# One pair of batch 1's queries and keys from TensorE transposes to DMA transposes, in a kernel of local attention and SwiGLU on one Trainium2 core

## The chip, the cores and the metric

The kernel runs on one core of one Trainium2 chip. The metric is device time in microseconds (us), taken over whole executions of the program; a second execution is recorded by the hardware profiler, and from it come the profile page and the trace. Lower is better. The engines of the core go by the profile's names: PE is TensorE (matrix products), PEld its weight loads, DVE is VectorE, ACT is ScalarE, POOL is GpSimd, SP is SyncE. POOL issues the loads that convert float32 to float16 on the way (software DMA); SP, and ACT for a few, issue the others.

## What is computed

An attention over 4 batches of 8 heads, 768 positions, 64 values per head, and a feed-forward block on its result. Each position sees the first 8 positions (the global keys) and the 96 positions up to itself:

```python
is_global = pos[None, :] < 8
is_local = (rel >= 0) & (rel < 96)          # rel = query position - key position
dist = np.where(is_global & ~is_local, 96.0, np.abs(rel))
scores = q @ k.T / 8 - slope[head] * dist    # slope = 2 ** -(head + 1)
scores = np.where(is_global | is_local, scores, -1e9)
a = softmax(scores)                          # over the keys, 1e-9 added to the sum
x = (a @ v) as (4 * 768, 8 * 64) = (3072, 512)
g = x @ w_gate                               # (512, 1536)
out = (g * sigmoid(g) * (x @ w_val)) @ w_out # (1536, 512), out (3072, 512) float32
```

Inputs and output are float32 in the chip's memory.

## The kernel before

**Staging.** Everything that TensorE multiplies is float16. Keys and queries must lie with the 64 values of a head across the partitions; two heads (a pair, `hp` 0 to 3) fill the 128 partitions. kT[hp] holds a pair's keys in 7 chunks of 120 with the 8 global keys ahead of each, qT holds its 768 queries. There are three ways to fill them:
- Batch 0 is loaded in halves of 384 positions and transposed on TensorE (`T`, tr_half, L360; products L364), then copied out of PSUM with a change of order (`k`, keys_half; `q`, queries_half, copy at L393). Its first pairs come as float32 through the queues of ACT and SP (`Lf`) and are cast (`cast`, L347).
- Pairs 0 and 1 of batch 1 come as two loads of four heads (`L4`, ld_four, L293) and are transposed on TensorE, 12 transposes for each call (`U`, tr_whole, L398; products L402), then copied out by `kw` (keys_whole, L406) and `qw` (queries_whole, L417).
- Pairs 2 and 3 of batch 1, and all of batches 2 and 3, come one head at a time by rows (`Lr.b.i.h`, ld_rows, L304, issued at L305; i is 0 for keys, 1 for queries). A DMA transpose on SP's queue (`D.b.hp.i`, tr_dma, L423, issued at L430) writes queries straight to qT and keys to kN, from which DVE spreads them into kT (`K`, spread_keys, L434).

The staging tiles, kst for keys and qst for queries, have two buffers each and are taken in turn by batch 0's float32, batch 0's float16, and batches 1, 2 and 3 (L290). Batch 3's first load of keys therefore goes into the buffer that batch 1's keys lie in, and waits for its last reader. kN and qT have four buffers each.

V comes in seven chunks per batch (`Lv.b.c`, ld_v, L264, issued at L267), with the V rows of the global keys copied into each chunk afterwards (`G`, put_globals; `G.1.1.7.S` is a DMA on SP that does chunks 1 to 6 of batch 1). The three vS tiles are cleared where no rows come (`Z`). The weights come in 256 KB pieces (`Lw.which.n.g`, ld_w, L312; which is 0 for w_gate, 1 for w_val) and w_out in three of 512 KB (`Lo`). `Lw.1.0.1` is the second half of the first 512 columns of w_val.

**Attention.** `c.b.hp.u` (scores, L481) multiplies keys by queries into two PSUM banks, `x` (exps, L526) takes the exponent on ACT into one of the at-buffers, `m` (mask, L553) multiplies by the mask on DVE. The masks hold exp(-slope * distance), made by ACT (`M.head.part`, L335); some units of batch 0 get the distance added by TensorE instead (`B`, L461, from `sl`). `w.b.g.half.what` (weigh, L571, products L585) sums over keys for four heads (g) and 384 queries (half): what 0 gives the sums of the weights, with `ones` (made by `pre`, L323) as left operand, 1 and 2 give even and odd columns of the weighted V. `i` (invert, transpose L604) and `r` (spread, L608) turn the sums into reciprocals in the right places, `n` (take_num, L597) copies weighted sums out of PSUM on ACT where the banks are wanted, and `p` (scaled, L621) writes the product, a quarter of a tile of x, transposed as xT.

**Feed-forward.** x is done in 8 tiles t of 384 positions, two per batch. For each of 12 blocks f of 128 columns there are four products with w_gate (`g.t.f`; `ga` and `gb` are its first and second half) and four with w_val (`v.t.f`), all at L638; ACT takes a tanh (`t`), DVE makes the rest of the gate (`s`) and the product with the value (`h`). `o.t.i.part` (L679, for the last rows L668) multiplies 128 rows by w_out, `e.t.i` (put_out) scales and stores them: on ACT and SP (L697), and for the last 128 rows e.7.2 on ACT's own queue and e.7.3 by DVE (L692) with the store on SP (L693).

**What sets the order.** Nothing is scheduled by the compiler. The string ORDER (L39 to L123) lists every step as name and arguments, the table WORK (L702) gives the function of each name, and the steps are issued in that order; each engine and each queue runs its own in order, waiting only for data and for buffers. The letter at the end of some steps is the engine: V is DVE, A is ACT, P is POOL, S is SP. The 8 PSUM banks are dealt by `single` and `double` in the order of the steps, so a moved step can also get another bank. `fill` (L343) runs products on a bank of no use, 14 and later 2, ahead of the first transposes.

```python
    for step in ORDER.split():
        name, *args = step.split(".")
        WORK[name](*(int(a) if a.isdigit() else a for a in args))
```

Batch 0's attention comes first, its second half among the first feed-forward tile; batch 1's loads are issued during tiles 0 and 1, its transposes, scores and sums stand in tile 1 and between tiles 1 and 2; batches 2 and 3 follow in the same way.

## Time and profile before

| | before |
|---|---|
| median of 3 runs | 238.46 us (238.38 to 238.53) |
| the profiled execution | 238.79 us, of it 237.0 from the first to the last instruction (the span) |
| granted TensorE clock | 1.0 |
| ACT: tanh (L644) | 96 instructions, 491 ns each, 44.1 us |
| DVE: gate (L648) and product (L654) | 96 each, 547 and 551 ns, 50.8 and 51.3 us |
| PE: products with w_gate and w_val (L638) | 384 each, 72.1 and 73.3 us |
| PE: products with w_out (L679) | 276, 68.5 us |
| DMA | 25.54 MB, 108 GB/s on the mean, 162 to 207 GB/s in the slices of the first quarter |
| V loads (Lv) | 24 of 120 KB, 8.0 us from issue to landing (median) |
| key and query rows (Lr) | 20 each, of 96 KB, 7.9 and 8.5 us |

In a row of the trace the first numbers are the start and the length in us, then come the engine, the line, the operation, the tile written and the tile read; "x4" is a group of four. What stands in square brackets is idle time of the engine ahead of the instruction and what ended it. In the chain of waits each row is a start, a length and a piece of work that the end of the span depended on. In a row by stretches of time the first column is the stretch and its length, followed by the busy times of PE, PEld, DVE, ACT, POOL and SP, the granted clock, and the DMA engines' load (the last number is GB/s). A queue's row ("SPq") is the issuing of a transfer; the transfer lands later, and a row of DMA issues gives the KB of each and the time from issue to landing. Times on POOL are rough.

### The profile page before, as it was taken

How to read it: one execution, taken by the hardware profiler on the slowest of the kernel's cores; microseconds unless marked ns; L12 is line 12 of the kernel's file. 1: busy time of each engine (PE TensorE's matmuls, PEld its weight loads, DVE VectorE, ACT ScalarE, POOL GpSimd, SP SyncE). 2: the span in 40 equal slices, each digit the busy share in tenths (PEclk: the TensorE clock that was granted, in tenths of full speed). 3: DMA queues.
4: the chain of work that ended last, by engine and by line, in shares of the span. 5: the costliest groups of instructions: out<-in, count | busy, mean ns of one | idle time of the engine just before them, and what ended most of it. 6: DMA issues, size and time to landing. Idle time of an engine off the chain costs nothing.

```text
span 237.0 us, 6183 instructions
## 1 busy us (share of the span) xinstructions
PE 229.5 (97%) x2520; PEld 132.3 (56%) x2520; DVE 173.8 (73%) x428; ACT 138.0 (58%) x251; POOL 77.6 (33%) x102
## 2 busy tenths in 40 slices
...
GB/s 177 181 182 207 193 198 186 176 176 162 139 130 153 178 165 139 141 167 112 139 192 55 44 80 27 20 47 47 0 44 48 3 1 0 44 47 0 8 125 177
DMA packets 88196, 25.54 MB, mean 108 GB/s; under 512 B 78016, under 2 KB 85224, under 8 KB 88168
## 3 DMA queue, kind: packets, MB, share of 16 engines
...
q8 instruction: 19, 0.31, 0.5%
...
## 4 chain that ended last, share of the span: by engine, by line
PE 94%; DVE 3%; ACT 1%; issue 1%; DVEq 0%
PE banks L638 53%; PE banks L679 26%; PE banks L585 6%; PE banks L481 4%; PE banks L343 2%; PE banks L668 1%; PE banks L364 1%; ACT at L526 1%; PE banks L461 1%; PE banks L402 1%; DVE at L518 0%; DVE rb L611 0%; DVE at L517 0%; DVE dT L604 0%; DVE xT L621 0%
## 5 line engine op out<-in xcount | busy, mean ns | idle before, releaser
L644 ACT ACTIVATE th<-banks 128x384 f32<-128x384 f32 x96 | 44.1, 491 | 60.1 <-PE banks L638 54.6
L638 PE MATMUL banks<-xT,wv 128*128 128x384 f16 x384 | 73.3, 326 | 0.0
L638 PE MATMUL banks<-xT,wg 128*128 128x384 f16 x384 | 72.1, 326 | 0.0
L654 DVE TENSOR_TENSOR hT<-banks,sl 128x384 f16<-128x384 f32 x96 | 51.3, 551 | 24.0 <-PE banks L638 22.2
L679 PE MATMUL banks<-wo,hT 128*128 128x512 f16 x276 | 68.5, 379 | 0.0
L526 ACT ACTIVATE at<-banks 64x640 f16<-64x640 f32 (+4 forms) x88 | 62.3, 714 | 5.3 <-PE banks L481 4.3
L648 DVE SCALAR_TENSOR_TENSOR sl<-th,banks 128x384 f32<-128x384 f32 x96 | 50.8, 547 | 12.6 <-ACT th L644 11.6
L638 PEld LDWEIGHTS <-wg 128*128 128x128 f16 x384 | 37.3, 98 | 27.0
L638 PEld LDWEIGHTS <-wv 128*128 128x128 f16 x384 | 36.4, 98 | 26.6
L679 PEld LDWEIGHTS <-hT 128*128 128x128 f16 x276 | 26.1, 98 | 26.5
L553 DVE TENSOR_TENSOR at<-at,masks 128x864 f16<-128x864 f16 (+5 forms) x62 | 26.1, 459 | 4.5 <-ACT at L526 4.4
L267 POOL DMA_DIRECT2D vS<-in_v_dram x28 | 25.0, 899 | 10.3 <-DMA vS<-in_v_dram 3.0
L697 ACT ACTIVATE osb<-banks 128x512 f32<-128x512 f32 x23 | 13.6, 597 | 22.1 <-PE banks L679 18.4
L305 POOL DMA_DIRECT2D kst<-in_k_dram x20 | 16.7, 841 | 14.1 <-DMA kN<-kst 8.8
L305 POOL DMA_DIRECT2D qst<-in_q_dram x20 | 16.8, 846 | 7.5 <-DMA qst<-in_q_dram 2.6
L481 PE MATMUL banks<-qT,kT 64*64 64x160 f16 (+9 forms) x408 | 13.3, 227 | 0.2 <-DVE xT L621 0.2
L481 PEld LDWEIGHTS <-kT 64*64 64x64 f16 (+1 forms) x408 | 7.9, 104 | 8.9 <-issue 7.6
L621 DVE TENSOR_TENSOR xT<-ns,rb 128x384 f16<-128x384 f32 x24 | 12.5, 550 | 0.3
L585 PE MATMUL banks<-at,vS 128*32 128x216 f16 (+6 forms) x576 | 12.0, 225 | 0.1
L597 ACT COPY ns<-banks 128x768 f32<-128x768 f32 x12 | 9.4, 801 | 4.5 <-PE banks L585 4.2
L604 DVE STREAM_TRANSPOSE dT<-banks 128x384 f32<-128x384 f32 x16 | 9.2, 574 | 3.1 <-PE banks L585 2.8
L585 PEld LDWEIGHTS <-vS 128*32 128x32 f16 x576 | 10.0, 95 | 2.3 <-issue 1.5
...
## 6 DMA issues: line engine op xcount, KB each, us to landing
out_dram<-osb SPq DMA_DIRECT2D x23, 256.0 KB, 2.1
...
qst<-in_q_dram POOLq DMA_DIRECT2D x20, 96.0 KB, 8.5
kst<-in_k_dram POOLq DMA_DIRECT2D x20, 96.0 KB, 7.9
wg<-in_moe_w_gate_dram POOLq DMA_DIRECT2D x6, 256.0 KB, 9.3
wv<-in_moe_w_val_dram POOLq DMA_DIRECT2D x6, 256.0 KB, 8.3
...
```

The source lines that it names most:

```text
L267: nc.gpsimd.dma_start(out=v_of(b)[r0:r0 + n, c, :, :], in_=v[b, :, KC * c:KC * c + n, :].rearrange("h p d -> p h d"))
L305: nc.gpsimd.dma_start(out=rows_of(i, b, h // 2)[:, :, h % 2, :], in_=KQ[i][b, h].rearrange("(t p) d -> p t d", p=128))
L481: nc.tensor.matmul(sc[k0:k1, hi, col + a:col + z], lhsT=keys[r, k0:k1], rhs=qTs[b, hp][r, q0 + a:q0 + z], start=fresh, stop=True, skip_gro ...
L526: nc.scalar.activation(out=of(at), in_=of(sc), func=AF.Exp, scale=scale)
L553: ENG[e].tensor_mul(a2, a2, m[:, :, m0:m0 + n])
L585: nc.tensor.matmul(dst[r, o:o + n], lhsT=vSs[b][:, c, 4 * g + j, what - 1::2] if what else ones[:, 0:32], rhs=ats[b, hp, u][:, j % 2, col: ...
L638: nc.tensor.matmul(gv[t, f, which][:, 0:TB], lhsT=w[:, c, 128 * f:128 * f + 128], rhs=xTs[t][:, c, :], start=(c == 0), stop=(c == NC - 1))
L644: nc.scalar.activation(out=th, in_=gv[t, f, 0][:, 0:TB], func=AF.Tanh, scale=0.5)
L648: nc.vector.scalar_tensor_tensor(out=sl, in0=gv[t, f, "t"], scalar=1.0, in1=gv[t, f, 0][:, 0:TB], op0=AluOp.add, op1=AluOp.mult)
L654: nc.vector.tensor_mul(hTs[t][:, f, :], gv[t, f, 1][:, 0:TB], gv[t, f, "s"])
L679: nc.tensor.matmul(ops_t[t, i], lhsT=hTs[t][:, f, 128 * i:128 * i + 128], rhs=wo[:, f, :], start=(f == 0), stop=(f == NFF - 1))
L697: nc.scalar.mul(out=osb, in_=ops, mul=0.5)
```

## The change

Pair 1 of batch 1 now takes the third way: its heads 2 and 3 come by rows (Lr.1.0.2, Lr.1.0.3, Lr.1.1.2, Lr.1.1.3), D.1.1.0 and D.1.1.1 transpose them by DMA, and K.1.1 spreads the keys. The steps U.1.0, U.1.1, kw.1 and qw.1 are gone, and so is n.1.1.0. Pair 0 alone stays on TensorE; its load takes two heads, not four.

```diff
-    def ld_four(i, h0):
+    def ld_pair(i, hp):
         nc.gpsimd.dma_start(
-            out=stage(1, i)[:, h0:h0 + 4, :],
-            in_=KQ[i][1, h0:h0 + 4].rearrange("h (p j) d -> p h (j d)", p=128))
+            out=stage(1, i)[:, 2 * hp:2 * hp + 2, :],
+            in_=KQ[i][1, 2 * hp:2 * hp + 2].rearrange("h (p j) d -> p h (j d)", p=128))
...
-        "G": put_globals, "Z": clear_rest, "L4": ld_four, "Lr": ld_rows,
+        "G": put_globals, "Z": clear_rest, "L2": ld_pair, "Lr": ld_rows,
```

The whole of ORDER is new. ORDER takes one line more, so the functions behind it stand one line lower than before (L638 is L639). Beside the steps above, these are the same steps at other places, but for the engine of five: cast.1.0 and k.3.1 go to DVE, q.1.0, q.0.0 and q.1.1 to ACT. What changes most:
- In the opening `pre` comes first. Seven of the sixteen masks (M.0.0, M.1.0, M.2.0, M.3.0, M.4.0, M.6.0, M.7.0), the clearing of the at-buffers' corners (zc.1, zc.2) and of two V tiles (Z.1, Z.2) go behind the first feed-forward products.
- On POOL's queue, Lr.3.0.1 stands ahead of Lv.1.1 to Lv.1.6; before, Lv.1.0, Lv.1.1, Lv.1.3 and Lv.1.2 stood ahead of it.
- On SP's queue, G.1.1.7.S stands behind D.2.0.0 and the stores e.0.0 and e.0.1.
- At the end e.7.2 stands ahead of e.7.1.

Of ORDER, the opening, the stretch in which batch 1 begins, and the end (some lines are left out at "..."):

```diff
-Ld.S Z.0.P Z.3.P Lf.A.1.1 Li zc.0.V Lh.0.0.4.8 zc.1.V Lf.A.1.0 Lh.1.0.4.8 pre cast.1.1.V Lf.S.0.1
-M.5.1 M.0.0 sl.3 Lf.S.0.0 M.2.1 Lh.1.1.0.4 fill.14 sl.7 M.1.0 sl.6 Lh.0.1.0.4 Z.1.V sl.2 cast.0.1.V
-M.7.0 T.1.0.1 B.1.1 q.1.0.V M.3.1 cast.1.0.P T.1.0.0 Lh.1.1.4.8 cast.0.0.A M.2.0 fill.2 Lv.0.1
-k.1.0.V sl.1 M.7.1 T.0.0.0 T.2.0.0 k.0.0.V Lv.0.0 T.3.0.0 sl.0 k.3.0.V M.4.1 M.5.0 B.1.0 M.0.1
-T.0.0.1 c.0.1.1 Lh.0.1.4.8 sl.4 T.2.0.1 M.3.0 c.0.1.0 q.0.0.V x.0.1.1 Lv.0.2 q.2.0.V T.1.1.1 T.3.0.1
-M.6.0 B.0.0 k.2.0.V x.0.1.0 Lv.0.3 c.0.0.0 sl.5 M.1.1 Lw.0.0.1 c.0.0.1 T.1.1.0 x.0.0.1 q.3.0.V M.4.0
-T.0.1.1 B.2.0 k.1.1.V c.0.2.0 Lw.0.0.0 B.3.1 x.0.0.0 Lw.1.0.0 x.0.2.0 Lw.1.0.1 M.6.1 T.0.1.0 q.1.1.V
-m.0.0.1.V w.0.0.0.0 Lw.0.1.0 B.3.0 k.0.1.V q.0.1.A c.0.3.1 x.0.3.1 c.0.2.1 c.0.3.0 i.0.0.0 Lw.0.1.1
-zc.2.V r.0.0.0 B.0.2 c.0.0.2 x.0.2.1 T.3.1.0 T.3.1.1 m.0.2.1.V T.2.1.1 x.0.3.0 Lw.1.1.1 w.0.1.0.0
-x.0.0.2 G.0.1.4.V k.3.1.A c.0.1.3 w.0.0.0.1 i.0.1.0 Lw.1.1.0 q.2.1.A w.0.0.0.2 T.2.1.0 w.0.1.0.1
-p.0.0.0.0.V x.0.1.3 w.0.1.0.2 r.0.1.0 k.2.1.A p.0.0.0.1.V c.0.2.2 Lw.0.2.0 c.0.0.3 q.3.1.A ga.0.0
-x.0.2.2 p.0.1.0.0.V ga.0.2 p.0.1.0.1.V G.0.4.7.S m.0.1.3.V c.0.1.2 x.0.0.3 c.0.2.3 Lw.0.2.1 Lv.0.6
-Lv.0.5 Lv.0.4 gb.0.2 x.0.1.2 gb.0.0 t.0.2 ga.0.1 m.0.2.2.V Lw.1.2.1 m.0.0.3.V gb.0.1 v.0.1 m.0.1.2.V
-w.0.0.1.0 s.0.2 t.0.0 s.0.0 c.0.3.3 Lw.1.2.0 x.0.2.3 i.0.0.1 c.0.3.2 v.0.0 g.0.3 t.0.1 x.0.3.3
...
-g.0.6 Lr.1.1.6 Lo.0 Lv.1.0 v.0.6 G.1.1.7.S Lv.1.1 m.0.2.3.V m.0.3.3.V Lo.1 h.0.1 v.0.5 s.0.7 t.0.6
-s.0.5 Lr.1.0.6 v.0.7 Lv.1.3 g.0.11 s.0.6 h.0.3 Lr.1.1.4 h.0.5 t.0.4 s.0.4 h.0.7 Lr.1.0.5 m.0.3.2.V
...
-v.0.9 p.0.1.1.1.V Lr.2.0.0 v.0.10 g.0.8 v.0.11 g.1.4 g.1.6 t.0.8 D.1.2.0 s.0.8 h.0.9 Lr.2.0.1 g.1.1
-h.0.10 t.1.4 t.1.1 h.0.2 g.1.8 s.1.4 g.1.5 s.0.11 U.0.0 U.0.1 D.1.2.1 s.1.1 U.1.1 t.1.8 U.1.0
-Lr.1.0.7 h.0.11 v.1.4 s.1.8 t.1.6 kw.0.A v.1.6 qw.1.A kw.1.V g.1.0 s.1.6 v.1.8 h.1.4 qw.0.A h.1.6
-t.1.0 Lv.1.2 s.1.0 c.1.0.1 c.1.1.0 v.0.8 g.1.9 t.1.5 h.1.8 x.1.1.0 s.1.5 t.1.9 x.1.0.1 v.1.1 g.1.2
-h.0.8 o.0.1.0 D.1.3.0 s.1.9 c.1.1.1 Lr.3.0.1 c.1.0.0 x.1.1.1 Lr.2.1.3 v.1.0 h.1.1 o.0.0.0 o.0.1.1
...
-h.1.11 o.0.0.3 s.1.3 h.1.9 o.0.1.3 m.1.1.0.V w.1.0.0.2 w.1.0.0.1 h.1.3 e.0.0 h.1.2 K.1.2 w.1.0.0.0
...
-Lr.2.1.5 o.0.2.1 o.0.2.2 h.1.5 t.1.10 Lv.1.4 c.1.3.1 p.1.0.0.0.V x.1.3.1 Lv.1.5 D.2.0.0 s.1.10
...
-w.1.0.1.1 w.1.0.1.0 w.1.0.1.2 t.2.5 Lr.3.1.4 Lv.2.4 s.2.5 s.2.0 w.1.1.1.1 e.1.1 w.1.1.1.0 Lv.2.0
...
-e.7.0 e.7.1 e.7.3 e.7.2
...
+pre Lf.A.1.0 Ld.S Li sl.5 sl.3 Lf.A.1.1 Z.3.P Z.0.P sl.2 cast.1.0.V fill.14 T.0.0.1 Lf.S.0.1 sl.4
+Lf.S.0.0 cast.1.1.V M.2.1 M.5.0 cast.0.1.V M.6.1 Lh.1.0.4.8 Lh.0.0.4.8 Lh.0.1.0.4 M.1.1 M.5.1
+T.1.0.1 sl.6 cast.0.0.A zc.0.V sl.1 sl.0 fill.2 Lh.0.1.4.8 Lh.1.1.4.8 sl.7 T.1.0.0 Lh.1.1.0.4 Lv.0.1
+B.1.1 Lv.0.0 M.3.1 B.1.0 q.1.0.A T.0.0.0 T.3.0.1 k.1.0.V q.0.0.A Lv.0.3 Lv.0.2 k.0.0.V c.0.1.1
+c.0.1.0 M.0.1 T.2.0.1 x.0.1.1 x.0.1.0 T.3.0.0 T.1.1.0 Lw.0.0.0 c.0.0.1 q.3.0.V k.3.0.V q.2.0.V
+T.0.1.0 x.0.0.1 Lw.0.0.1 M.4.1 B.0.0 Lw.1.0.0 c.0.0.0 B.3.1 c.0.3.1 x.0.0.0 T.2.0.0 m.0.0.1.V
+T.2.1.1 B.2.0 Lw.1.0.1 Lw.0.1.0 q.2.1.A x.0.3.1 Lw.0.1.1 M.7.1 w.0.0.0.0 k.1.1.V k.2.0.V T.0.1.1
+T.3.1.0 k.0.1.V q.0.1.A Lw.1.1.1 c.0.2.1 Lw.1.1.0 T.1.1.1 Lw.0.2.0 i.0.0.0 k.3.1.V G.0.1.4.V x.0.2.1
+Lw.0.2.1 T.3.1.1 c.0.2.0 B.3.0 q.1.1.A Lv.0.5 B.0.2 q.3.1.A Lv.0.6 Lv.0.4 c.0.3.0 c.0.0.2 m.0.2.1.V
+r.0.0.0 x.0.2.0 G.0.4.7.S x.0.3.0 T.2.1.0 w.0.0.0.2 w.0.1.0.0 c.0.1.3 x.0.0.2 p.0.0.0.1.V k.2.1.A
+c.0.0.3 w.0.0.0.1 i.0.1.0 x.0.0.3 w.0.1.0.1 p.0.0.0.0.V w.0.1.0.2 r.0.1.0 c.0.1.2 Lw.1.2.0 ga.0.0
+x.0.1.3 p.0.1.0.0.V ga.0.2 x.0.1.2 c.0.2.2 c.0.3.2 Lw.1.2.1 p.0.1.0.1.V x.0.2.2 Lr.1.1.2 m.0.1.2.V
+gb.0.0 ga.0.1 x.0.3.2 M.0.0 Lr.1.1.3 gb.0.2 g.0.3 Lr.1.1.6 Lr.2.0.1 v.0.3 Lr.1.0.4 L2.1.0 v.0.0
+gb.0.1 t.0.0 t.0.2 t.0.3 m.0.2.2.V m.0.1.3.V m.0.0.3.V s.0.0 t.0.1 s.0.2 s.0.3 c.0.2.3 c.0.3.3 h.0.0
...
+p.0.1.1.1.V p.0.1.1.0.V g.1.6 h.0.5 g.1.8 Lr.2.0.0 g.1.2 h.0.2 h.0.9 Lo.2 Lr.1.1.4 D.1.1.0 h.0.11
+v.0.8 t.1.8 D.1.1.1 D.1.2.0 g.1.1 g.1.4 t.1.2 s.0.8 v.1.2 h.0.10 s.1.8 s.1.2 D.1.2.1 g.1.0 v.1.4
+h.0.8 h.1.2 v.1.6 M.1.0 M.7.0 D.1.3.0 t.1.1 v.1.1 t.1.6 t.1.0 s.1.6 U.0.1 D.1.3.1 U.0.0 Z.1.V h.1.6
+o.0.1.0 s.1.1 M.4.0 s.1.0 Lv.1.0 M.2.0 t.1.4 g.1.11 s.1.4 Lr.3.0.1 v.1.0 kw.0.A o.0.1.1 h.1.1 Lv.1.1
+t.1.11 qw.0.A M.3.0 s.1.11 h.1.0 g.1.3 v.1.8 h.1.4 g.1.5 Lv.1.2 zc.2.V c.1.0.1 h.1.8 g.1.9 g.1.7
+Lv.1.3 o.0.0.0 t.1.3 t.1.7 Lr.2.0.5 zc.1.V Lr.2.0.2 s.1.3 Lr.2.1.2 v.1.3 o.0.0.1 Lr.3.0.2 s.1.7
+Lr.2.0.3 x.1.0.1 Lv.1.4 v.1.9 t.1.5 c.1.0.0 m.1.0.1.V t.1.9 Lr.2.0.4 x.1.0.0 s.1.5 o.0.0.2 K.1.1
+D.2.0.0 Lr.2.1.3 o.0.0.3 o.0.1.2 Lv.1.6 h.1.3 c.1.1.0 v.1.5 s.1.9 e.0.0 m.1.0.0.V Lr.2.1.4 o.0.1.3
+Lv.1.5 v.1.11 Lr.2.1.6 K.1.2 x.1.1.0 M.6.0 c.1.2.1 c.1.2.0 h.1.9 e.0.1 h.1.11 h.1.5 g.1.10 G.1.1.7.S
...
+m.1.3.0.V o.1.0.2 Lr.2.0.7 w.1.1.0.0 w.1.0.0.0 i.1.1.0 Lv.2.6 x.1.0.2 i.1.0.0 w.1.1.0.1 D.2.1.0
...
+m.1.1.2.V w.1.0.1.2 t.2.10 t.2.5 s.2.10 w.1.1.1.0 w.1.0.1.0 t.2.9 s.2.5 s.2.9 w.1.0.1.1 w.1.1.1.1
...
+h.7.11 o.7.2.0 e.5.1 o.7.0.3 o.7.2.1 o.7.1.1 o.7.1.2 e.6.0 o.7.1.3 o.7.2.2 e.7.0 e.7.2 e.7.1 o.7.2.3
+e.7.3
```

115 lines of the change are left out of this document (57 added, 58 removed).

## The prediction

> **What bounds the kernel now.** I read the page first (busy times, then the chain that ended last), then that chain in order of time, then who waited for whom.
>
> ```profile
> span 237.0 us, 6183 instructions
> ...
> PE 229.5 (97%) x2520; PEld 132.3 (56%) x2520; DVE 173.8 (73%) x428; ACT 138.0 (58%) x251; POOL 77.6 (33%) x102
> ...
> PE 94%; DVE 3%; ACT 1%; issue 1%; DVEq 0%
> ```
> ```profile
> 20.74 0.76 PE banks L638 x4
> ...
> 42.25 1.46 PE banks L402 x48
> ...
> 58.46 0.65 PE banks L638 x4
> ...
> 69.12 0.92 PE banks L585 x48
> ...
> 80.63 1.95 PE banks L585 x120
> ...
> 233.97 0.29 DVE osb L692
> ```
> ```profile
> PE banks L343 <- DVE ones L323: 3.8, 1, 3.8
> PE banks L461 <- ACT at L526: 0.3, 1, 0.3
> PE banks L481 <- DVE xT L621: 0.2, 1, 0.2
> ```
>
> TensorE (PE) is busy for 229.5 of 237.0 us, and in the chain every piece from 20.74 (the first feed-forward product) to 233.97 is a PE piece. PE waits only three times, never after 21 us. So the end is the start of this stretch, plus its PE work, plus a tail. A change can do three things: take PE work out, start the stretch at another time, or open a hole in it. The other engines matter only where they do the last two.
>
> The span is 237.0; the profiled execution took 238.79, so 1.8 lie around the span. The median of the runs is 238.46, 0.33 below. I sum against the span and subtract from the median.
>
> **The transposes that go: -0.73.** The L402 row of the chain is all of batch 1's TensorE transposes, 48 in 1.46 us. Pair 1's 24 (U.1.0, U.1.1) go: 0.73, sitting in the gapless stretch, so it is full gain. Their copies out of PSUM go too (qw.1 on ACT, kw.1 on DVE), K.1.1 comes to DVE, and n.1.1.0 leaves ACT. Seven masks and the clearing of at-buffers and of V's corners move from the opening into the first feed-forward tiles.
>
> ```profile
> 24.00:60.00 36.00, 36.00 (x393) 21.56 (x390) 29.55 (x67) 18.91 (x37) 18.57 (x24) 1.00 1.60 178
> ```
>
> In this stretch PE (first column after the length) is busy 36.00 of 36 us, DVE 29.55, ACT 18.91: 6 and 17 us are free, and each moved piece costs these engines under 3 us. I price them at nothing; if DVE had no room, it would be up to 3.
>
> **The opening: -0.35.** PE does the same steps ahead of ga.0.0, the first product, in both orders, but for c.0.2.2 against c.0.1.2. So the start is read from ACT, which in the new order carries five more query copies and seven masks fewer ahead of x.0.3.0, the exponent on which the last sum of the first half waits.
>
> ```profile
> L526 ACT ACTIVATE at<-banks 128x864 f16<-128x864 f32 x6 | 5.3, 910 | 0.0
> L335 ACT ACTIVATE masks<-dist 128x432 f16<-128x432 f16 x8 | 4.3, 554 | 0.2 <-DMA dist<-dist_c 0.2
> ...
> L526 ACT ACTIVATE at<-banks 128x336 f16<-128x336 f32 x4 | 1.7, 450 | 1.1 <-PE banks L481 1.1
> L393 ACT COPY qT<-banks 128x384 f16<-128x384 f16 x3 | 1.7, 552 | 0.0
> ```
> ```profile
> 7.00 0.51 ACT L347 CAST k<-k 128x384 f16<-128x384 f32 x1 [1.47 <-DMA k<-in_k_dram]
> ```
> ```profile
> 15.76 2.08 ACT L526 ACTIVATE at<-banks 128x336 f16<-128x336 f32 x4
> ...
> 17.43 0.44 PE L585 MATMUL banks<-at,ones 128*32 128x216 f16 x16
> ...
> 18.14 0.56 DVE L604 STREAM_TRANSPOSE dT<-banks 128x384 f32<-128x384 f32 x1
> ...
> 18.88 0.53 DVE L621 TENSOR_TENSOR xT<-banks,rb 128x384 f16<-128x384 f32 x1
> ...
> 20.67 0.82 PE L638 MATMUL banks<-xT,wg 128*128 128x384 f16 x4
> ```
>
> From the cast at 7.00, which waits for its load in both orders, ACT runs the cast (0.51), four masks of 432 (2.22), six query copies (3.31), four exponents of 336 (1.80) and four of 864 (3.64): 11.48, so x.0.3.0 ends at 18.5 if nothing overlaps. The row at 15.76 shows overlap: four exponents of 450, 450, 910 and 650 ns in 2.08, 0.095 saved at each; 18 times that is 1.7, and the end is 16.8 without a wait. With waits for PE like the 1.1 in the rows I take 17.9. Before, the sum that needs it (w.0.1.0.0) ran at 17.43. Behind x.0.3.0 the new order has w.0.1.0.0 (0.44), transpose and reciprocal (0.74, from 18.14 to 18.88), one product p.0.0.0.0 (0.53), c.0.1.2 and ga.0.0, some 0.3 to 0.6: 2.4 us, where the old order took 3.24 from 17.43 to 20.67, since it queued more ahead of that product. So ga.0.0 comes at 20.3: -0.35. The ends are 19.2 and 20.9 by this sum (16.8 or 18.5, plus 2.4). Another limit ends almost at the same place:
>
> ```profile
> 13.21 0.72 POOL L312 DMA_DIRECT2D wv<-in_moe_w_val_dram  x1 [0.20 <-issue]
> ```
> ```profile
> wv<-in_moe_w_val_dram POOLq DMA_DIRECT2D x1, 256.0 KB, 8.5
> ```
>
> This piece of w_val lands at 21.7 and is the fourteenth GpSimd (POOL) load in both orders. v.0.3 needs it and stands 2.6 us of PE work behind ga.0.0, so a ga.0.0 before 19.1 would only wait there: -1.55 at most.
>
> **The tail: +0.15.** e.7.2 now goes ahead of e.7.1.
>
> ```profile
> 234.30 0.33 SPq L693 DMA_DIRECT2D out_dram<-osb  x1
> ```
>
> This is the issue of the last store (e.7.3) on SyncE (SP). e.7.1's store, also on SP, now comes so late, behind e.7.2's multiply on ACT, that its issue, of the same kind and about the same 0.33, can stand in front of the last one: 0 to 0.33, I take the middle.
>
> **A new wait: +0.4.** The order moves one step past others on POOL's queue. Lr.3.0.1 writes the buffer that batch 1's key transposes read, so it waits until D.1.3.0 has landed; POOL is in order. Before, four V loads of batch 1 stood ahead of it; now Lv.1.1 to Lv.1.6 all stand behind.
>
> ```profile
> 50.49 1.33 SPq L430 DMA_TRANSPOSE kN<-kst  x1
> 52.01 1.22 SPq L430 DMA_TRANSPOSE qT<-qst  x1
> 55.12 1.21 SPq L430 DMA_TRANSPOSE kN<-kst  x1
> ...
> 61.52 1.52 SPq L430 DMA_TRANSPOSE kN<-kst  x1
> ```
> ```profile
> 58.84 0.83 POOL L305 DMA_DIRECT2D kst<-in_k_dram  x1 [8.78 <-DMA kN<-kst]
> ...
> 60.54 1.65 POOL L305 DMA_DIRECT2D kst<-in_k_dram  x2
> ```
> ```profile
> 34.00:56.00 22.00, 22.00 (x288) 13.61 (x288) 17.29 (x40) 13.94 (x26) 10.32 (x13) 1.00 1.82 177
> ```
>
> Landing times, from the issue rows: of the transposes at 50.49 and 55.12,
> ```profile
> kN<-kst SPq DMA_TRANSPOSE x1, 6.2
> ```
> ```profile
> kN<-kst SPq DMA_TRANSPOSE x1, 3.2
> ```
> of the two loads at 60.54 (least, median, most), then of those at 72.24 and 73.05,
> ```profile
> DMA to landing us min/median/max: 7.6/7.8/8.1
> ```
> ```profile
> DMA to landing us min/median/max: 7.7/7.7/7.8
> ```
>
> When does D.1.3.0 land? The DMA engines are full here, at 177 GB/s. The twenty-fifth load lands at 33.9 in both orders (issued at 25.88, 8.0 to landing):
> ```profile
> 25.88 0.72 POOL L312 DMA_DIRECT2D wv<-in_moe_w_val_dram  x1 [0.56 <-DMA wv<-in_moe_w_val_dram]
> ```
> Behind it the new order has, up to Lr.1.1.4, fourteen rows of 96 KB, two pairs of 192 and three blocks of 512: 3.34 MB, 18.9 us, so 52.8; two transposes of 0.2 MB beside them make it up to 55.0, I take 54.2. D.1.2.1 waits for that, D.1.3.0 is issued 1.5 later (the spacing of 50.49 and 52.01), at 55.7, and lands 3.2 later at 58.9. Before it landed at 58.3, so POOL restarts 0.6 later.
>
> Counted from the restart, Lv.1.3 is the fourth load and Lv.1.5 the fifteenth. Before, the fourth landed at 69.4 (the second of the two at 60.54, issued at 61.35, 8.1 to landing) and the fifteenth, the second of the next two, at 80.8 (issued at 73.05, 7.7). To these: +0.6 for the restart; +0.4 since three more of the loads are of 120 KB; -1.1 for D.2.0.0, which goes before the restart and no longer into the middle of them (0.2 MB at 177); for the fifteenth -1.1 again, since D.2.1.1 comes later. That is 69.3 and 79.6. PE wants them at w.1.1.0.1 and w.1.0.1.2. w.1.1.0.1 started in the group at 69.12, at 69.34; by the steps ahead of it (two more output parts at the 0.65 of such a group of PE, +1.3; U.1 and two sums fewer, -1.3; the opening, -0.35) it now comes at 69.0. w.1.0.1.2 was at 81.2 and comes at 79.5 (one product more, one fewer, U.1, two sums, -0.35). The slack that was over 4 us is gone: 0.3 of wait at the first, then 79.6 against 79.8. I take 0.4 in all. Sure to either side is only 0 (both loads a microsecond earlier) to 3: a transpose under load takes 6.2, not 3.2.
>
> The copy of the global keys' V rows (G.1.1.7.S), which before was issued at 42.8, stands behind D.2.0.0 and two stores on SP now, at about 61.5; with the 6.2 of a transpose under load it still lands before 69 (estimated).
>
> **Sum.** -0.73 - 0.35 + 0.15 + 0.4 = -0.53: span 236.5, time 237.9.
>
> **Rivals.**
> - *Opening at its limit, no wait.* ga.0.0 at 19.1: -0.73 - 1.55 + 0.15 = -2.1, 236.3. For it: ACT's sum without waits allows 19.2. Against: ACT does wait for PE in the rows. 0.10.
> - *No wait for V.* The two loads land a microsecond sooner: 0.4 less, 237.5. For it: the transpose issued at 55.12, with no loads queued, took 3.2, and two of the new order's six start earlier than any did before. Against: 6.2 beside loads. 0.15. The Trainium skill, DMA: Bandwidth & Descriptors, section Queues, rings and completion order, has each DMA engine go round the queues packet by packet; by that a transpose always gets its turn beside a full load queue, D.1.3.0 is early and this rival comes true. The two rows agree with it only in part.
> - *V behind the key transposes* (slower). D.1.3.0 takes 6.2, because the transposes queue behind one another and beside the last loads. Each microsecond that it lands after 58.9 is one more of wait at w.1.1.0.1 or w.1.0.1.2; from 0.9 on the change loses. Full price 3.0: 240.9; half of it 239.4. For it: the row at 50.49, and no slack left. Against: at 55.12 the load queue was empty, as it will be. 0.30.
> - *The opening stays slow.* PE starts its 14 filling matmuls as soon as `ones` is set, now DVE's first work, and then idles until the first cast.
> ```profile
> 8.74 1.08 PE L364 MATMUL banks<-ident,k 128*64 128x128 f16 x18
> ...
> 11.27 0.53 PE L364 MATMUL banks<-ident,q 128*64 128x128 f16 x12
> ```
> Before, 18 transposes at 8.74 took 60 ns each, 12 at 11.27 took 44. If the hole kept PE at the slower pace for another 3 us, these would take 60/44 as long, 1.1 more, of which half may be hidden: 238.4 to 239.0. 0.08. The Trainium skill, TensorE: Matmul & The Clock Gate, Part 1, has the array at full clock after some 3.4 us of sustained work, in windows that run freely; by it the hole can cost one window.
> - *The gain is eaten.* PE needs DVE's last product of the second half (p.0.1.1.0) within about a microsecond, and the like elsewhere; 0.5 of it lost: 238.4. 0.06.
>
> **Chances.** The forecast itself has 0.31 (237.6 to 238.4, half of it under 237.98). What a measurement of this kernel can tell from no change is about 0.2%, 0.48 us. Faster: 0.10 + 0.15 + 0.16 = 0.41. Same: 0.15 + 0.06 + 0.02 of the slow opening = 0.23. Slower: 0.30 + 0.06 = 0.36. The range leaves out about a tenth at each end: 236.7 to 240.2.
>
> **What would show it.** In the chain one L402 group of 24, 0.73. First L638 at 20.3 (19.1 to 20.9). Who waited: a PE row for L585 released by a DMA of vS near 69 or 80; none would mean 237.5, one over 1.5 us the second rival. The restart of POOL's L305 at 59.4. At the end L693 0.15 later behind PE. I am wrong altogether if PE waits anywhere else for over 0.5 us.

## The result and the profile after

The changed kernel takes 239.97 us (median of 4 runs, 239.54 to 240.31); the kernel before took 238.50 beside it. The ratio is 1.006 with a 95% interval of 1.0035 to 1.0084: slower, where I had forecast 0.2% faster. The profiled execution took 239.54 with a span of 237.8, so 0.8 over the one before; it is the quickest of the four. Of all runs below, one is left out as a slow one, 247.08 us of a_v_first.

The first lines of the page of the changed kernel (span, busy time of each engine, the engines' shares in the chain that ended last):

```profile
span 237.8 us, 6162 instructions
PE 231.2 (97%) x2496; PEld 131.7 (55%) x2496; DVE 172.2 (72%) x429; ACT 137.9 (58%) x249; POOL 79.6 (33%) x105
PE 86%; ACT 6%; DVE 3%; DMA 2%; issue 1%; SPq 0%; DVEq 0%; ACTq 0%
```

PE has 24 matmuls fewer than before and is busy for 1.7 us more, so its busy time holds small delays too; the chain, which was 94% PE, now holds DVE and ACT. Its rows, in order of time:

```profile
19.89 0.76 PE banks L639 x4
...
45.44 0.79 PE banks L403 x24
...
50.27 0.56 DVE hT L655
51.00 0.15 DVE at L519
...
52.92 0.56 DVE sl L649
53.53 0.81 PE banks L639 x4
...
58.27 0.70 ACT at L527
...
69.54 0.71 ACT at L527
70.29 0.99 PE banks L586 x39
```

The first product came 0.85 sooner than in the chain before (20.74), and the transposes that are left take 0.79 where 1.46 stood. Then, at 50.3, the chain leaves PE: DVE clears corners (L518, L519) and only then makes the gate (L649) that frees the bank for PE's next product. Who waited for whom on PE (total, times, longest):

```profile
PE banks L344 <- DVE ones L324: 1.2, 1, 1.2
PE banks L365 <- DVE q L348: 0.5, 1, 0.5
PE banks L365 <- DVE k L348: 0.4, 1, 0.4
PE banks L639 <- DVE sl L649: 0.3, 1, 0.3
```

No row names a DMA of V, the wait that I had priced. The row of L639 is the one at 53.53. The same shows in the stretch from 50 to 56, first of the kernel before, then of the changed one (PE is the first column after the length, DVE the third):

```profile
50.00:56.00 6.00, 6.00 (x49) 3.41 (x49) 3.20 (x9) 4.51 (x9) 0.07 (x1) 1.00 1.83 162
```
```profile
50.00:56.00 6.00, 5.67 (x45) 2.77 (x44) 4.65 (x21) 2.80 (x7) 0.00 (x0) 1.00 1.55 196
```

A second stretch of the chain is not on PE: from 58.3 to 70.3 it goes through ACT, mostly exponents (L527), up to the sums of batch 1 (L586). ACT is the fourth column from 56 to 75, before and after:

```profile
56.00:75.00 19.00, 19.00 (x255) 10.22 (x254) 14.27 (x38) 14.13 (x22) 14.25 (x19) 1.00 1.79 149
```
```profile
56.00:75.00 19.00, 18.87 (x262) 9.54 (x261) 13.89 (x35) 16.37 (x25) 14.74 (x18) 1.00 1.64 163
```

Before, the chain was on PE there. By this chain, PE time saved in that stretch alone would turn at least in part into waiting for ACT; no run tests that by itself.

**The sum of the 0.8.** For each PE step I take the time from its start to the start of the next one, less the median of that for steps of its kind in the kernel before: what is over is a wait or a dearer change from one kind to the next. From the first product to the start of the last step this adds up to 2.90 before and 4.64 after (both shift with how finely the kinds are told apart, their difference does not). All of the difference, 1.74, lies between 50 and 75 us (0.63 before, 2.37 after). So:

| | profile after | second profile of the same kernel (a_again) |
|---|---|---|
| start of the first product, against before | -0.85 | +0.62 |
| steps of PE at the medians of before (two transposing steps fewer) | -0.69 | -0.69 |
| waits and changes of kind, all between 50 and 75 | +1.74 | +1.74 |
| from the start of the last PE step to the end (3.57 before) | +0.55 | +0.54 |
| sum, and the difference of the spans | +0.75 | +2.21 |

The second column is the same kernel profiled once more. The three rows in the middle repeat to 0.01; the opening differs by 1.5. From the first product to the end of the span it is 216.34 before, 217.94 and 217.93 in the two profiles after. So the loss has a fixed part of 1.6, and an opening that comes up to 0.9 sooner or later from one execution to the next.

### The profile page after: what moved, and what is told of

The parts are those of the page before. It is cut to its first block, busy times and chain, and to the rows that moved or that the text cites. A ratio compares the mean times of both kernels' runs of the same rounds, so it can differ in the third digit from the quotient of the medians.

```text
span 237.8 us, 6162 instructions
## 1 busy us (share of the span) xinstructions
PE 231.2 (97%) x2496; PEld 131.7 (55%) x2496; DVE 172.2 (72%) x429; ACT 137.9 (58%) x249; POOL 79.6 (33%) x105
## 4 chain that ended last, share of the span: by engine, by line
PE 86%; ACT 6%; DVE 3%; DMA 2%; issue 1%; SPq 0%; DVEq 0%; ACTq 0%
PE banks L639 51%; PE banks L680 23%; PE banks L586 6%; ACT at L527 5%; PE banks L482 4%; DMA k<-in_k_dram 2%; PE banks L669 1%; PE banks L365 1%; DVE kT L378 1%; ACT qT L394 0%; PE banks L462 0%; ACT osb L698 0%; ACT masks L336 0%; PE banks L403 0%; DVE at L519 0%
## 5 line engine op out<-in xcount | busy, mean ns | idle before, releaser
L639 PE MATMUL banks<-xT,wv 128*128 128x384 f16 x384 | 74.6, 326 | 0.3 <-DVE sl L649 0.3
L639 PE MATMUL banks<-xT,wg 128*128 128x384 f16 x384 | 73.9, 326 | 0.1
L680 PE MATMUL banks<-wo,hT 128*128 128x512 f16 x276 | 69.3, 380 | 0.0
L527 ACT ACTIVATE at<-banks 64x640 f16<-64x640 f32 (+4 forms) x88 | 61.9, 713 | 8.0 <-PE banks L482 6.9
L649 DVE SCALAR_TENSOR_TENSOR sl<-th,banks 128x384 f32<-128x384 f32 x96 | 50.5, 546 | 12.2 <-ACT th L645 11.4
L639 PEld LDWEIGHTS <-wv 128*128 128x128 f16 x384 | 37.1, 98 | 28.0 <-issue 0.6
L639 PEld LDWEIGHTS <-wg 128*128 128x128 f16 x384 | 36.6, 98 | 26.4
L306 POOL DMA_DIRECT2D kst<-in_k_dram x22 | 18.5, 853 | 17.8 <-PE banks L680 11.5
L698 ACT ACTIVATE osb<-banks 128x512 f32<-128x512 f32 x23 | 13.6, 597 | 15.9 <-PE banks L680 13.7
L306 POOL DMA_DIRECT2D qst<-in_q_dram x22 | 18.6, 857 | 4.8 <-DMA kst<-in_k_dram 2.0
L482 PE MATMUL banks<-qT,kT 64*64 64x160 f16 (+9 forms) x408 | 14.2, 229 | 0.1
L598 ACT COPY ns<-banks 128x768 f32<-128x768 f32 x11 | 8.6, 800 | 6.2 <-PE banks L586 3.9
L586 PE MATMUL banks<-at,vS 128*32 128x216 f16 (+6 forms) x576 | 12.1, 225 | 0.0
L622 DVE TENSOR_TENSOR xT<-ns,rb 128x384 f16<-128x384 f32 x22 | 11.2, 546 | 0.3
L586 PEld LDWEIGHTS <-vS 128*32 128x32 f16 x576 | 10.0, 95 | 2.3 <-issue 1.8
```

The costliest lines, as they stand in the source:

```text
L306: nc.gpsimd.dma_start(out=rows_of(i, b, h // 2)[:, :, h % 2, :], in_=KQ[i][b, h].rearrange("(t p) d -> p t d", p=128))
L482: nc.tensor.matmul(sc[k0:k1, hi, col + a:col + z], lhsT=keys[r, k0:k1], rhs=qTs[b, hp][r, q0 + a:q0 + z], start=fresh, stop=True, skip_gro ...
L527: nc.scalar.activation(out=of(at), in_=of(sc), func=AF.Exp, scale=scale)
L586: nc.tensor.matmul(dst[r, o:o + n], lhsT=vSs[b][:, c, 4 * g + j, what - 1::2] if what else ones[:, 0:32], rhs=ats[b, hp, u][:, j % 2, col: ...
L639: nc.tensor.matmul(gv[t, f, which][:, 0:TB], lhsT=w[:, c, 128 * f:128 * f + 128], rhs=xTs[t][:, c, :], start=(c == 0), stop=(c == NC - 1))
L649: nc.vector.scalar_tensor_tensor(out=sl, in0=gv[t, f, "t"], scalar=1.0, in1=gv[t, f, 0][:, 0:TB], op0=AluOp.add, op1=AluOp.mult)
```

## Experiments

My theory after the first result: the clearing in DVE's queue, more changes between kinds of matmul on PE, and the end. Its rivals: the V loads stand right behind and would take over what the clearing gives back, or the engine named has no room anyway.

Runs in us; "first product" and "span" are of the profiled execution, "first product" the start of ga.0.0.

| run | median (n, lowest to highest) | ratio to before (95%) | first product | span |
|---|---|---|---|---|
| a_again | 240.84 (6, 239.61 to 241.54) | 1.0087 (1.0062 to 1.0112) | 21.29 | 239.2 |
| a_clear | 240.13 (8, 238.70 to 241.26) | 1.0061 (1.0038 to 1.0085) | 21.59 | 239.0 |
| a_tail | 239.71 (8, 238.91 to 241.34) | 1.0047 (1.0025 to 1.0070) | 20.73 | 238.5 |
| a_both | 240.69 (6, 239.47 to 241.31) | 1.0075 (1.0051 to 1.0098) | 21.00 | 238.6 |
| b_split | 240.63 (6, 239.89 to 240.88) | 1.0074 (1.0059 to 1.0090) | 20.61 | 238.8 |
| a_warm | 239.53 (9, 239.01 to 240.41) | 1.0047 (1.0030 to 1.0064) | 20.67 | 238.6 |
| a_warm2 | 239.65 (12, 238.73 to 240.76) | 1.0045 (1.0029 to 1.0062) | 19.67 | 237.8 |
| a_load | 239.64 (10, 238.59 to 241.38) | 1.0044 (1.0018 to 1.0071) | 20.46 | 238.0 |
| b_cold | 239.12 (12, 238.55 to 240.34) | 1.0032 (1.0016 to 1.0048) | 20.61 | 237.0 |
| h_batch1 | 241.57 (4, 241.35 to 241.78) | 1.0128 (1.0114 to 1.0141) | 20.45 | 239.8 |
| h_opening | 242.66 (6, 241.60 to 243.76) | 1.0173 (1.0148 to 1.0198) | 19.69 | 239.8 |
| h_batch1_end | 242.81 (4, 242.51 to 243.07) | 1.0179 (1.0166 to 1.0192) | 20.65 | 241.3 |
| a_v_first | 243.96 (5, 242.37 to 245.47) | 1.0223 (1.0185 to 1.0261) | 19.77 | 242.2 |

The kernel before, run beside a_clear, a_tail, b_split and a_both, took 238.12 to 239.13 in 15 runs: a spread of 1.0. No version of the changed order beat it.

### a_clear: the clearing on another engine

```diff
-Lv.1.0 ... zc.2.V ... Lr.2.0.5 zc.1.V Lr.2.0.2
+Lv.1.0 zc.1.P ... zc.2.V ... Lr.2.0.5 Lr.2.0.2
```

> The changed kernel, with one step moved: the clearing of the at-buffers' corners for unit 1 (zc.1, ten memsets, 2.1 us on DVE at 50.8) goes to POOL, right behind Lv.1.0, where POOL idles from 48.8 to 60.3. My theory (clearing in DVE's queue holds up the gate product s.1.3, so v.1.3 finds no bank): PE's wait of 0.5 at 52.9 goes, with up to 0.35 of later small waits; span 237.8 becomes 237.0 to 237.3. Rival 1 (the V loads are the limit right behind it, Lv.1.3 landed at 68.9): PE comes to w.1.1.0.1 earlier and waits there, the gain is 0.2 at most, span 237.6. Rival 2 (DVE is simply full there): the wait turns up at another product, span unchanged.

Measured: the wait is gone. PE in the stretch from 50 to 56 of this kernel:

```profile
50.00:56.00 6.00, 6.00 (x42) 3.20 (x40) 3.30 (x8) 3.02 (x6) 1.44 (x8) 1.00 1.56 157
```

The extra spacing of PE falls from 4.64 to 4.16, and from the first product to the end of the span it is 217.45 where two profiles of the changed kernel have 217.94 and 217.93. So the clearing cost 0.5, and no V wait took its place. But the median did not fall, and the span is 1.3 longer: this profile's first product came at 21.59. That was the first sign that the opening, untouched by this edit, is not the same from one execution to the next.

### a_tail: the old end

```diff
-o.7.2.0 e.5.1 o.7.0.3 o.7.2.1 o.7.1.1 o.7.1.2 e.6.0 o.7.1.3 o.7.2.2 e.7.0 e.7.2 e.7.1 o.7.2.3 e.7.3
+e.5.1 o.7.0.3 o.7.1.1 o.7.1.2 o.7.2.0 e.6.0 o.7.1.3 o.7.2.1 o.7.2.2 e.7.0 o.7.2.3 e.7.1 e.7.3 e.7.2
```

> The changed kernel, with the end put in the old order: o.7.1.1 to o.7.1.3 ahead of o.7.2.1 and e.7.1 ahead of e.7.2, so that the store of 256 KB of e.7.1 goes out about 1 us before the last store and not 0.44 before it. My theory (the last landing stands behind that store's 256 KB): from the start of the last PE step to the end 3.56 us as before, not 4.16; span 237.8 becomes 237.2. Rival (only the issue on SP counts, the 0.15 of my prediction): span 237.6 to 237.7.

Measured: from the start of the last PE step to the end of the span 3.93, where it was 4.12 in the changed kernel and 3.57 before (the 4.16 and 3.56 above are from rounded spans). So the order of the last stores is worth 0.2, not 0.6. In the changed kernel the two stores were issued like this:

```profile
234.12 0.33 SPq L699 DMA_DIRECT2D out_dram<-osb  x1
234.25 0.29 DVE L693 TENSOR_SCALAR osb<-banks 128x128 f32<-128x128 f32 x1 [7.02 <-PE banks L669]
234.56 0.37 SPq L694 DMA_DIRECT2D out_dram<-osb  x1
```

From this last issue to the end it is 3.19, before 2.72, in a_tail 3.00. Where the other 0.36 of the 0.55 comes from isn't settled: a_tail puts the last three stores in the old order, but not the stores of tile 6, which were also moved.

### b_split: the price of a run of scores

```diff
-c.1.0.1 c.1.1.0 v.0.8
+c.1.0.1 v.0.8 c.1.1.0
...
-c.2.0.1 c.2.0.2 t.3.7 Lr.3.1.5 s.3.7 x.2.0.1 v.2.10
+c.2.0.1 v.2.10 c.2.0.2 t.3.7 Lr.3.1.5 s.3.7 x.2.0.1
```

(and six more of the kind)

> The kernel before, with eight pairs of neighbouring score steps taken apart, one feed-forward step of PE between the two of each pair (c.1.1.0, c.1.0.0, c.2.1.0, c.2.0.2, c.2.2.0, c.2.3.0, c.3.2.1, c.3.3.2 are the second ones). The same work, eight more runs of scores on PE. My theory (each run of scores costs PE about 0.09 going in and 0.02 to 0.10 going out, 0.2 in all, read from the spacing of steps): span 237.0 becomes 238.3 to 238.8. Rival (the spacing is an artefact of how ends of matmuls are recorded): 237.0 to 237.2.

Measured: span 238.8, 1.8 over the kernel before, extra spacing 4.74 against 2.90: 0.23 for each of the eight. One of them in the timeline of PE, first in the kernel before, then split:

```profile
100.66 0.50 PE L481 MATMUL banks<-qT,kT 64*64 64x160 f16 x20
101.09 0.82 PE L638 MATMUL banks<-xT,wv 128*128 128x384 f16 x4
101.75 0.49 PE L638 MATMUL banks<-xT,wg 128*128 128x384 f16 x2
```
```profile
101.28 0.33 PE L481 MATMUL banks<-qT,kT 64*64 64x160 f16 x8
101.55 0.82 PE L638 MATMUL banks<-xT,wv 128*128 128x384 f16 x4
102.30 0.36 PE L481 MATMUL banks<-qT,kT 64*64 64x168 f16 x12
102.60 1.47 PE L638 MATMUL banks<-xT,wg 128*128 128x384 f16 x8
```

The same 24 matmuls take 1.09 (100.66 to 101.75) together and 1.32 (101.28 to 102.60) apart. The changed order has nine runs of scores in batch 1, the old one six; two of the new ones are c.1.0.0 and c.1.1.0, which no longer stand beside another pair's scores. Three runs at 0.23 are 0.7. That is a price carried over from one kernel to another, not a saving that was measured.

### a_both: all repairs, and one run of scores less

```diff
-c.1.2.2 p.1.1.0.0.V ... o.1.1.2 c.1.1.2 ... c.1.3.2
+c.1.2.2 p.1.1.0.0.V ... c.1.1.2 ... c.1.3.2 o.1.1.2
```

(with the edits of a_clear and a_tail)

> The changed kernel with both repairs of the two runs beside it (clearing on POOL, the old end), and o.1.1.2 moved behind c.1.3.2, so that c.1.2.2, c.1.1.2 and c.1.3.2 are one run. My theory: 0.5 to 0.85 for the clearing, 0.6 for the end, 0.2 for the run less: span 237.8 becomes 236.2 to 236.5, time about 238.1, 0.2 under the kernel before. Rival (the V loads limit): 236.8 to 237.0, no better than before.

Measured: the join cost more than it gave. In the joined run c.1.3.2 stood 0.51 over its usual spacing for a PSUM bank that DVE's product (L622) had still to read, and the extra spacing is 4.49 where clearing and join should have left 3.9. From the first product to the end it is 217.60, 0.34 less than in the changed kernel, and the clearing and the end alone are worth 0.7. The median is that of the changed kernel; again the opening came late (21.00).

### a_again: the changed kernel once more

> The changed kernel once more, as it is, beside the others. In its first profile the first product came at 19.82; in the profiles of three kernels with the same opening it came at 20.73, 21.00 and 21.59, and their runs spread over 1.8 to 2.6 us where those of the kernel before spread over 1.0. My theory now (TensorE idles between the filling matmuls and the first casts, and its pace then depends on chance): the runs spread over 1.5 us or more, and in the profile the first product comes somewhere from 19.8 to 21.6 with the groups of six transposes at 0.53 us up to that much later. Rival (the opening is as steady as before, and the three edits moved it): spread under 1 us, first product at 19.8.

Measured: spread 1.9, first product at 21.29. The rows of PE show why. In the changed kernel's first profile, then in this one:

```profile
4.87 1.14 PE L365 MATMUL banks<-ident,q 128*64 128x128 f16 x12 [0.51 <-DVE q L348]
...
8.51 0.53 PE L365 MATMUL banks<-ident,k 128*64 128x128 f16 x6
...
11.02 0.36 PE L365 MATMUL banks<-ident,k 128*64 128x128 f16 x6
```
```profile
4.87 0.36 PE L365 MATMUL banks<-ident,q 128*64 128x128 f16 x6 [0.51 <-DVE q L348]
...
6.93 0.36 PE L365 MATMUL banks<-ident,k 128*64 128x128 f16 x6 [0.77 <-DVE k L348]
...
7.98 0.53 PE L365 MATMUL banks<-ident,k 128*64 128x128 f16 x6
8.81 0.53 PE L365 MATMUL banks<-ident,q 128*64 128x128 f16 x6 [0.29 <-ACT qT L394]
```

Six transposes take 0.53 when PE is slow and 0.36 when it is fast. In the first profile PE was slow at 4.87 and fast at 11.0; in the second it was fast at 4.87 already, idled, and was slow from 8 to beyond 14. The stretches of the second profile (granted clock third from the end):

```profile
4.00:8.00 4.00, 2.47 (x30) 1.02 (x28) 3.12 (x14) 1.85 (x5) 4.00 (x6) 0.97 1.25 192
8.00:14.00 6.00, 5.71 (x70) 3.39 (x72) 4.09 (x16) 4.63 (x9) 4.77 (x7) 0.50 1.84 176
```

PE was busy 2.47 of 4 us, and then got half the clock for 6 us. The Trainium skill, TensorE: Matmul & The Clock Gate, Part 1, has in its table of the two states the array go to full clock after a window of about 3.4 us with work and back after one without, and the windows run freely, not from the kernel's start. The free-running window agrees: the same instructions at the same times, and another pace. That the fall back takes a whole window without work does not: PE's idle stretches here were 0.8 at most, with 2.47 of 4 us busy, and it fell back all the same.

The clock granted over whole executions says the same. Of the 32 executions of the changed kernel (both times), a_clear, a_tail and a_both, which open alike, eight were granted 0.986, and all eight took 240.76 us or more; of the other 24 three did. None of 67 executions of the kernel before, run beside the experiments, was granted less than 0.998.

### b_cold: the early fill in the kernel before

```diff
-Ld.S Z.0.P ... Lh.1.0.4.8 pre cast.1.1.V
+pre Ld.S Z.0.P ... Lh.1.0.4.8 cast.1.1.V
```

> The kernel before, with one step moved: pre, which sets the ones, stands first, so that the 14 filling matmuls run from 1.2 to 4.4 and TensorE then idles for 2 us up to the first transposes. Nothing else of the change. My theory: its runs spread over 1.5 us or more and the median rises by 0.5 to 1.5; in the profile groups of six transposes take 0.53 us beyond 10.2, where they take 0.36 in the kernel before. Rival: DVE's two first casts come 0.7 sooner, the fill costs nothing, the time is 238.2 to 238.6.

Measured: this one step, moved alone, makes the kernel before 0.3% slower (1.0016 to 1.0048) and widens its runs to 1.8, where 26 of the kernel before beside it spread over 1.1. PE idles where it was busy, and the clock shows it (first the kernel before, then this run):

```profile
4.00:8.00 4.00, 4.00 (x30) 2.70 (x28) 3.00 (x12) 2.53 (x8) 4.00 (x6) 1.00 1.32 200
8.00:14.00 6.00, 5.91 (x89) 3.33 (x86) 5.54 (x24) 4.90 (x12) 5.80 (x9) 1.00 1.87 175
```
```profile
4.00:8.00 4.00, 2.14 (x31) 1.15 (x30) 3.71 (x14) 2.60 (x9) 4.00 (x6) 1.00 1.28 201
8.00:14.00 6.00, 5.91 (x79) 3.04 (x75) 5.07 (x22) 5.17 (x12) 5.47 (x8) 0.72 1.86 178
```

The profiled execution itself came out even (first product 20.61); one of the twelve was granted 0.986 of the clock and was the slowest (240.34). The harm is a matter of chance.

### a_warm: fill in the holes

```diff
-fill.14 T.0.0.1 ... fill.2 ... T.0.0.0
+fill.17 T.0.0.1 ... fill.5 ... fill.2 T.0.0.0
```

> The changed kernel with more filling matmuls in the holes of the opening: 17 in place of 14 at the start, 5 in place of 2 behind T.1.0.1, and 2 more ahead of T.0.0.0, so that TensorE hardly idles up to 8.5 us. My theory: the first product comes at 19.8 to 20.2 (0.2 for fill that stands in the way), the spread of the runs falls under 1 us, the median by 0.5 to 1.2 against the changed kernel run beside it. Rival (the pace is set by something else, the holes don't matter): spread and median as the changed kernel's, or 0.3 slower for the fill.

Measured: 239.53 against 240.84 for the changed kernel run beside it, 1.3 less, and no run above 240.41. The intervals of these two ratios just touch, and against the first four runs of the changed kernel (239.97) it is only 0.4 less: a gain is likely, its size is not settled. None of the nine was granted less than 0.999 of the clock, where three of the six beside it had 0.986. The spread is still 1.4. In this profile PE is fast from 6.6 on, but the first product came at 20.67 all the same. PE waited for DVE, and DVE (second fence) for a V load:

```profile
PE banks L586 <- DVE vS L279: 1.3, 1, 1.3
```
```profile
16.80 0.94 DVE L279 COPY vS<-vS 8x1536 f16<-8x1536 f16 x1 [1.73 <-DMA vS<-in_v_dram]
```

The copy of the global keys' V rows needs Lv.0.0, which landed at 13.6 in the kernel before and at 16.8 here. The new order has one half load of keys more in front of it, but in the changed kernel's first profile, with the same order of loads, it landed at 15.0; the 1.7 more here are another difference between executions. So the opening has a second limit, in the loads.

### a_warm2: fill, clearing and end together

```diff
-fill.14 ... fill.2 ... T.0.0.0 ... Lv.1.0 ... zc.1.V
+fill.17 ... fill.5 ... fill.2 T.0.0.0 ... Lv.1.0 zc.1.P
```

(with the end of a_tail)

> The kernel of the run a_warm, with the clearing of zc.1 on POOL (which took 0.6 of PE's 0.85 us of delay in the stretch from 50 to 56 away in the run a_clear) and the old end (0.2 in the run a_tail). My theory: the three causes add up: 0.8 under a_warm, 238.0 to 238.5, level with the kernel before or 0.2 under it. Rival: the clearing's 0.6 comes back as a wait for V, 0.2 under a_warm.

Measured: 239.65, no better than a_warm: the rival held. With the opening early (19.67) and the clearing out of the way, PE came to the sums of batch 1 before their V. Who waited, and the row:

```profile
PE banks L586 <- DMA vS<-in_v_dram: 1.2, 2, 0.6
```
```profile
70.51 0.67 PE L586 MATMUL banks<-at,vS 128*32 128x24 f16 x28 [0.56 <-DMA vS<-in_v_dram]
```

Here is the wait that I had predicted: 0.56 at w.1.1.0.1 for Lv.1.3, which landed at 70.47. (The other 0.6 is batch 0's V at 16.3.)

### a_v_first: V ahead of the load that waits

```diff
-Lr.3.0.1 v.1.0 ... Lv.1.1 ... Lv.1.5 v.1.11
+v.1.0 ... Lv.1.1 ... Lv.1.5 Lr.3.0.1 v.1.11
```

(on top of a_warm2)

> The kernel of a_warm2 with Lr.3.0.1 moved on POOL's queue from ahead of Lv.1.1 to behind Lv.1.5, so that no V load of batch 1 waits for the key transposes. In the profile of a_warm2 PE waited 0.56 at w.1.1.0.1 for Lv.1.3, landed at 70.5. My theory (the new wait of my prediction, hidden in the changed kernel because PE came there late, and real as soon as PE is early): that wait is gone, Lv.1.3 lands before 60, and the median falls by 0.2 to 0.6 against a_warm2, 239.65. Rival: the V loads now run beside the transposes of pairs 1 to 3, D.1.1.0 lands over 1 us later, PE or ACT waits for K.1.1 instead, no gain.

Measured: the rival held, and far beyond its numbers: 4.3 slower. Who waited on PE:

```profile
PE banks L482 <- DMA qT<-qst: 3.5, 2, 3.3
```

The V loads, and three loads of batch 2's rows behind them, now run beside the transposes of pairs 1 to 3. Time to landing of D.1.2.0 and D.1.2.1, two rows of this kernel, then two of a_warm2:

```profile
kN<-kst SPq DMA_TRANSPOSE x1, 8.1
```
```profile
qT<-qst SPq DMA_TRANSPOSE x1, 7.6
```
```profile
kN<-kst SPq DMA_TRANSPOSE x1, 4.7
```
```profile
qT<-qst SPq DMA_TRANSPOSE x1, 2.8
```

So Lr.3.0.1 ahead of the V loads, which I had read as a new wait, is also what keeps the transposes quick.

### h_batch1 and h_opening: the two halves of the new order

```diff
-(h_batch1) ga.0.0 and all ahead of it in the new order
+(h_batch1) ga.0.0 and all ahead of it in the old order, with c.0.1.2 for c.0.2.2
...
-(h_opening) all behind ga.0.0 in the new order
+(h_opening) all behind ga.0.0 in the old order; zc.2.V, zc.1.V and the masks between the steps of tiles 0 and 1
```

> A cross of the two orders: every step up to the first product ga.0.0 in the order of the kernel before (masks and clearing in the opening with it), every step behind it in the order of the changed kernel, with pair 1 by DMA. So the opening is undone and the new stretch of batch 1 stays. Nothing else differs but two steps' places in the dealing of PSUM banks. My theory: the opening is steady again (first product at 20.5 to 20.8, runs spread over 1.1 us at most), no wait at v.1.3; against the kernel before -0.7 for the transposes, +0.8 for three more runs of scores, +0.35 for two small waits on ACT, +0.4 at the end: 0.8 slower, 239.2 to 239.6. Rival (all of the loss sits in the opening and the clearing): 0.7 faster, 237.8.

> The other cross: up to the first product in the order of the changed kernel, behind it in the order of the kernel before, with pair 1's transposes on TensorE and the old end; the masks and the clearing that the old opening held are put between the first tiles' steps (clearing of zc.1 behind s.0.8 on DVE). My theory: the opening alone brings the spread (1.5 us or more) and costs 0.3 to 1.2 in the median, 238.8 to 239.7; in the profile the first product comes anywhere from 19.8 to 21.6. Rival (the opening is a gain of 0.85, as in the first profile of the changed kernel): 237.7 to 238.0.

Measured: both are slower than either kernel, and neither is a clean half; a few loads and steps near the seam also stand elsewhere than in either order. In h_batch1 the seam costs 2.0 in new waits between 20 and 40 us, 0.9 of them right behind the first product. Between 50 and 75, with the clearing and the masks back in the opening, its extra spacing is 1.7, where the changed kernel has 2.4 and the one before 0.6: the clearing's part is gone there, and over 1.0 is left for the order of batch 1 itself. What can be read is the spread: 0.43 in 4 runs with the old opening, 2.2 in 6 runs with the new one. And h_opening priced the clearing once more, at another place. Its rows of DVE (eight like the first two are left out) and of PE:

```profile
39.68 0.15 DVE L517 MEMSET at<- 64x112 uint32 x1
39.90 0.15 DVE L518 MEMSET at<- 64x112 uint32 x1
...
41.78 1.49 DVE L654 TENSOR_TENSOR hT<-banks,sl 128x384 f16<-128x384 f32 x3
```
```profile
42.39 0.81 PE L638 MATMUL banks<-xT,wg 128*128 128x384 f16 x4 [1.84 <-DVE hT L654]
```

The same ten memsets cost PE 0.5 at 50.8 and 1.84 at 39.7, where three products stood ready behind them in DVE's queue.

### h_batch1_end

```diff
-v.1.9 t.1.5 c.1.0.0 m.1.0.1.V t.1.9 Lr.2.0.4 x.1.0.0 s.1.5 o.0.0.2 K.1.1 ... c.1.1.0
+v.1.9 t.1.5 m.1.0.1.V t.1.9 Lr.2.0.4 s.1.5 o.0.0.2 K.1.1 c.1.0.0 x.1.0.0 c.1.1.0 ...
```

(on top of h_batch1, with the end of a_tail; c.1.1.0 comes forward too, by two output parts)

> The kernel of h_batch1 with the old end and one run of scores less (c.1.0.0 moved down to stand beside c.1.1.0, behind K.1.1). My theory: 0.2 for the run and 0.2 to 0.4 for the end, 238.7 to 239.1. Rival: the score that comes later makes ACT late, no gain.

Measured: its rival held. c.1.1.0 waited 1.6 for the banks that c.1.0.0, now late, still held. In these two joins, here and in a_both, what the run saved was lost again to waits for PSUM banks that ACT and DVE still held.

### a_load: batch 0's V

```diff
-Lv.0.1 B.1.1 Lv.0.0 ... T.2.1.0 w.0.0.0.2 w.0.1.0.0 c.0.1.3
+Lv.0.0 Lv.0.1 B.1.1 ... T.2.1.0 w.0.1.0.0 w.0.0.0.2 c.0.1.3
```

(on top of a_warm2)

> The kernel of a_warm2 (more fill, clearing on POOL, old end) with two steps of the opening moved: the load Lv.0.0 ahead of Lv.0.1, and the sum w.0.0.0.2, which reads V, behind w.0.1.0.0, which reads no V. With a warm PE the opening was then held by batch 0's V: in the profile of a_warm the copy G.0.1.4 stood for Lv.0.0 (landed 16.8, 13.6 in the kernel before) and the first product came at 20.67; in that of a_warm2 w.0.0.0.2 stood 0.7 for Lv.0.2 (landed 17.2) and it came at 19.67. My theory (the pace of PE and batch 0's V loads together make the spread): the first product at 19.2 to 19.8, spread under 1.2 us, median 239.0 to 239.3 against 239.65. Rival (the spread is all from PE's pace, or from the weights' loads behind): spread 1.5 to 2 as in a_warm2, median 239.5 to 239.8.

Measured: 239.64, spread 2.8, first product 20.46. The theory fell: V alone does not make the rest of the spread. In this profile DVE's second cast waited 0.9 for its load, and PE stood 1.1 for the cast: the very first loads vary too. PE was busy for only 2.69 us from 4 to 8 and kept the full clock (1.00 from 8 to 14), so a hole makes the slow pace possible and not certain.

## Why the prediction was wrong

The forecast had -0.73 for the transposes, -0.35 for the opening, +0.15 for the end and +0.4 for waits between. The first profile has -0.69, -0.85, +0.55 and +1.74. So it is the last term that turned the sum round, and none of it was the wait that I had priced.

**The transposes: right.** -0.73 was forecast; the chain's group went from 1.46 to 0.79, PE's steps from 209.87 to 209.18.

**"I price them at nothing": the step that failed.** Seven masks and the clearing were moved "into the first feed-forward tiles", where DVE had 6 us free out of 36. The room was there, but a block of 2.1 us in an in-order queue does not spread itself over it: the next gate product stood behind it, and PE's bank behind that. It cost 0.5 (a_clear), and 1.84 where it stood at a worse place (h_opening). My bound of 0 to 3 held it, the value of 0 was wrong. The same line gave ACT 17 us free from 24 to 60; it did not look at 58 to 70, where the chain then ran on ACT.

**Runs of scores: a term that was missing.** I counted the steps of PE and not in what order their kinds follow one another. Three more runs of scores in batch 1 are 0.7 of the 1.74 at the price of b_split, 0.23 each; that the kernel would be faster by this without them is not shown, since both joins lost it again. Two waits for ACT, 0.15 behind an output copy (L698) and 0.20 behind an exponent (L527), were not foreseen either; the last 0.2 of the 1.74 I can't assign.

**The opening: -0.35 was one draw of many.** It came 0.85 sooner in one profile and 0.6 later in the other. My rival "the opening stays slow" had the mechanism, PE idling between its fill and the first cast, and its place; but I gave it 0.08 and took the outcome as one number, where it is a lottery in each execution. That the first profile was sooner still than my 20.3 was luck. Filling PE's holes took 0.4 to 1.3 us off (a_warm); moving the fill alone cost the old kernel 0.3% (b_cold). With the fixed 1.6 this makes medians of 1.5 and 2.3 over the kernel before.

**The end: +0.15 was 0.55**, of which the order of the last stores is 0.2 (a_tail); the rest is open. The later issue that I had priced is 0.07 of it (0.93 from the start of PE's last step to the last issue, 0.86 before); the rest lies behind that issue.

**The wait for V: +0.4 was nothing here, for a reason that the forecast did not have.** Its own working came out close. The time to landing of D.1.3.0, issued at 55.65, and of Lv.1.2 and Lv.1.3 (median):

```profile
kN<-kst SPq DMA_TRANSPOSE x1, 3.5
```
```profile
vS<-in_v_dram POOLq DMA_DIRECT2D x2, 120.0 KB, 6.1
```

D.1.3.0 landed at 59.1 (58.9 forecast), POOL went on at 60.3 (59.4; what held it for the last 1.1 isn't shown), Lv.1.3 landed at 68.9 (69.3) and Lv.1.5 at 78.8 (79.6), 1.9 before PE wanted it. PE came to w.1.1.0.1 only at 69.8, since it had lost 0.5 to the clearing and more to the runs. Where the clearing is gone and PE is early the wait is real: 0.56 in a_warm2, 0.3 in a_load. The slower rival, "V behind the key transposes", came near the right time, 239.4 for half of it, for the wrong reason: by luck.
